# Fused cosformer attention and low-rank mixer: half-head opening, full-array tails, and DMA transposes from batch 2 on

## The chip, the cores and the metric

The kernel runs on one core of one Trainium2 chip. The core has TensorE (PE: matmuls and, on a line of its own, weight loads), VectorE (DVE), ScalarE (ACT), GpSimd (POOL) and SyncE (SP), which here issues the DMAs. The metric is the device time of one execution in microseconds; the time before is the median of three runs.

## The reference

Per batch (8) and head (8), with S = 576 positions and D = 64:

```
r   = max(q or k, 0);  phi = [r * cos(pi/2 * s/S), r * sin(pi/2 * s/S)]      # 128 features
kv  = phi(k)^T v  (128 x 64);   z = sum over s of phi(k)
x   = phi(q) kv / (phi(q) z + 1e-6)                                         # heads side by side: S x 512
A   = U^T x   (32 x 512);   u = x + V^T A
out = u + max(u w1, 0) w2                                                   # w1 512 x 2048, w2 2048 x 512
```

Inputs and output are float32, matmul operands bf16.

## The kernel before

**Tiling.** The 576 positions of a batch are four chunks of 128 (position 4p + c lies on partition p of chunk c) and a tail of 64. Tails of an even batch lie on partitions 0 to 63, of an odd one on 64 to 127, so that two batches, a pair, share one 128-row tail in the MLP. Each batch goes through these units, each a function:

- `load` (L398): six DMAs on SP, a tail and a main part each for k, v and q. k has two buffers, v and q one.
- `k_prep` (L188, on VectorE), `q_prep` (L199, on ScalarE): a cosine and a sine pass per chunk, max(x, 0) times a weight per position. `v_prep` (L173, on GpSimd) casts v and leaves a column of ones, so that kv carries z in column 65.
- `kv_unit` (L210): for four heads, five matmuls each (four chunks and the 64-row tail) into one PSUM tile, cast on VectorE.
- `qtr_unit` (L231): eight TensorE transposes of a chunk of q's features into the PSUM tile T, copied on VectorE to q_pT.
- `x_unit` (L243): eight matmuls of a transposed chunk with kv, then add, reciprocal and multiply on VectorE.
- `A_unit` (L276), `u_unit` (L290): U^T x (a 128 x 32 shape, 64 x 32 for the tail), then V^T A (32 rows) and the add of x on VectorE.
- `utr_unit` (L308): four transposes of u per chunk into T, copied to uT.
- `g1_main` (L327): one of 16 column blocks of the first MLP layer, four matmuls of 512 columns, evicted by ScalarE with a relu into hid (three PSUM buffers g). `g1_tail` (L343): the same for the pair's tail, four blocks at a time. `g2_part` (L364): a quarter of an output chunk's 16 matmuls into o (two PSUM buffers); after the fourth, VectorE adds u (L386) into one of three o_sb buffers, and SP stores it.

PSUM has eight banks: g three, T one, X two (one buffer of two banks), o two.

**Order.** The schedule is manual: each engine and each DMA queue runs its instructions in program order. The opening (L444 to L489) does batch 0 in two halves of four heads, then A, u and transposes, then all 16 `g1_main` of batch 0, and then batch 1's prep, attention and mixer. After that a loop over four pairs (L491) runs 72 MLP slots per pair (`mlp_slots`, L433: 16 and 16 `g1_main`, 4 `g1_tail`, 36 `g2_part`; pair 0 starts at slot 16). Behind a slot it runs the units that `put` has hung there for the next pair's batches: `pe_plan` (L409) gives each unit of a batch an offset, `prep_plan` (L424) those of the prep passes, and `starts` the slot at which a batch begins and the number of slots over which its 36 offsets are spread: (22, 47, 24) in pair 0, (0, 37, 35) later. The next `load` is hung 8 slots behind a batch's start, or at slot 71.

Of the kernel before, what the change touches and what calls it, by code (L numbers as in the profile page):

```python
# [17 lines left out]
def kernel(  # L18
# [14 lines left out]
    H = 8  # L33
# [136 lines left out]
    k_p, q_p, q_pT, kv_sb, x_bf, x_tl, A_sb = {}, {}, {}, {}, {}, {}, {}  # L170
    u_bf, u_tl, uT, uT_tl = {}, {}, {}, {}

    def v_prep(b, h0=0, h1=H):  # L173
        vx = v_ext[b % 2]
        for c in range(4):
            nc.gpsimd.tensor_copy(out=vx[:, c, h0:h1, 0:D], in_=vst[b][:, h0:h1, c, :])  # L176
        if h0 == 0:
            nc.gpsimd.tensor_copy(out=vx[tail(b), 4, :, 0:D], in_=vt[b][tail(b)])
# [9 lines left out]
    def k_prep(b, c, eng, h0=0, h1=H, half=None):  # L188
        if b not in k_p:
            k_p[b] = pool.tile([P, 5, H, 2 * D], BF16, tag="k_p", bufs=1, name="k_p")  # L190
        rows = slice(0, P) if c < 4 else tail(b)
        src = kst[b][:, h0:h1, c, :] if c < 4 else kt[b][rows, h0:h1, :]
        for i, w in enumerate((cosw, sinw)):
            if half in (None, i):
                scaled_relu(
                    eng, k_p[b][rows, c, h0:h1, i * D : i * D + D], src, w[rows, c : c + 1]
                )

    def q_prep(b, c, eng, h0=0, h1=H, half=None):  # L199
        if (b, c) not in q_p:  # L200
            q_p[b, c] = pool.tile([P, H, 2 * D], BF16, tag="q_p", bufs=5, name="q_p")
        rows = slice(0, P) if c < 4 else tail(b)
        src = qst[b][:, h0:h1, c, :] if c < 4 else qt[b][rows, h0:h1, :]
        for i, w in enumerate((cosw, sinw)):
            if half in (None, i):
                scaled_relu(
                    eng, q_p[b, c][rows, h0:h1, i * D : i * D + D], src, w[rows, c : c + 1]
                )

    def kv_unit(b, hg, tag, bufs):  # L210
# [4 lines left out]
        for i in range(4):  # L215
            h = hg * 4 + i
            for c in range(5):
                rows = slice(0, P) if c < 4 else tail(b)
                nc.tensor.matmul(  # L219
                    out=acc[:, i, :],  # L220
                    lhsT=k_p[b][rows, c, h, :],
                    rhs=vx[rows, c, h, :],
                    start=(c == 0),
                    stop=(c == 4),
                )
        nc.vector.tensor_copy(out=kv_sb[b][:, hg * 4 : hg * 4 + 4, :], in_=acc)  # L226

    def cols(c):
        return slice(c * P, c * P + P) if c < 4 else slice(512, S)

    def qtr_unit(b, c, h0=0, h1=H, eng=None):  # L231
        if b not in q_pT:
            q_pT[b] = pool.tile([P, H, S], BF16, tag="q_pT", bufs=1, name="q_pT")
        n = P if c < 4 else TS
        rows = slice(0, P) if c < 4 else tail(b)
        t_ps = ps.tile([P, H, P], BF16, tag="T", bufs=1, name="t_ps")
        for h in range(h0, h1):
            nc.tensor.transpose(  # L238
                out=t_ps[:, h, 0:n], in_=q_p[b, c][rows, h, :], identity=ident[rows, rows]
            )  # L240
        cast(eng or nc.vector, q_pT[b][:, h0:h1, cols(c)], t_ps[:, h0:h1, 0:n])

    def x_unit(b, c, hgs, tag, bufs):  # L243
        if b not in x_bf:
            x_bf[b] = pool.tile([P, 4, DM], BF16, tag="x_bf", bufs=1, name="x_bf")
            x_tl[b] = pool.tile([P, DM], BF16, tag="x_tl", bufs=1, name="x_tl")
        n = P if c < 4 else TS
        rows = slice(0, P) if c < 4 else tail(b)
        ng = len(hgs)
        acc = ps.tile([P, ng, 512], FP32, tag=tag, bufs=bufs, name="x_ps")  # L250
        for g, hg in enumerate(hgs):
            for i in range(4):
                h = hg * 4 + i
                nc.tensor.matmul(  # L254
                    out=acc[rows, g, i * E : i * E + E],
                    lhsT=q_pT[b][:, h, cols(c)],
                    rhs=kv_sb[b][:, h, :],
# [3 lines left out]
        view = acc[rows, :, 0 : 4 * E].rearrange("p g (i e) -> p g i e", e=E)  # L261
        rec = pool.tile([P, ng, 4], FP32, tag="rec", bufs=2, name="rec")
        nc.vector.tensor_scalar(
            out=rec[rows], in0=view[:, :, :, D], scalar1=1e-6, scalar2=None, op0=ALU.add
        )
        nc.vector.reciprocal(out=rec[rows], in_=rec[rows])
        dst = x_bf[b][:, c, :] if c < 4 else x_tl[b][rows, :]
        dst = dst[:, hgs[0] * 256 : hgs[0] * 256 + ng * 256]
        nc.vector.tensor_tensor(  # L269
            out=dst.rearrange("p (g i d) -> p g i d", g=ng, d=D),  # L270
            in0=view[:, :, :, 0:D],
            in1=rec[rows].unsqueeze(3).to_broadcast([n, ng, 4, D]),
# [3 lines left out]
    def A_unit(b, tag, bufs):  # L276
        A_sb[b] = pool.tile([R, DM], BF16, tag="A_sb", bufs=2, name="A_sb")
        a_ps = ps.tile([R, DM], FP32, tag=tag, bufs=bufs, name="a_ps")
        for c in range(5):
            rows = slice(0, P) if c < 4 else tail(b)  # L280
            nc.tensor.matmul(  # L281
                out=a_ps,
                lhsT=U_bf[rows, c, :],
                rhs=x_bf[b][:, c, :] if c < 4 else x_tl[b][rows, :],
# [3 lines left out]
        nc.vector.tensor_copy(out=A_sb[b], in_=a_ps)  # L288

    def u_unit(b, c, tag, bufs):  # L290
        if b not in u_bf:
# [4 lines left out]
        n = P if c < 4 else TS  # L296
        va = ps.tile([P, DM], FP32, tag=tag, bufs=bufs, name="va_ps")
        nc.tensor.matmul(  # L298
            out=va[rows, :], lhsT=V_bf[:, c, 0:n], rhs=A_sb[b], start=True, stop=True
        )  # L300
        nc.vector.tensor_tensor(  # L301
            out=u_bf[b][:, c, :] if c < 4 else u_tl[b // 2][rows, :],
            in0=x_bf[b][:, c, :] if c < 4 else x_tl[b][rows, :],
# [3 lines left out]

    def utr_unit(b, c, eng=None):  # L308
        if b not in uT:
            uT[b] = pool.tile([P, 4, 512], BF16, tag="uT", bufs=2, name="uT")  # L310
            if b % 2 == 0:
                uT_tl[b // 2] = pool.tile([P, 4, P], BF16, tag="uT_tl", bufs=2, name="uT_tl")
        rows = slice(0, P) if c < 4 else tail(b)
        n = P if c < 4 else TS
        t_ps = ps.tile([P, H, P], BF16, tag="T", bufs=1, name="t_ps")
        for d in range(4):
            src = u_bf[b][:, c, :] if c < 4 else u_tl[b // 2][rows, :]
            nc.tensor.transpose(  # L318
                out=t_ps[:, d, 0:n], in_=src[:, d * P : d * P + P], identity=ident[rows, rows]
            )  # L320
        dst = uT[b][:, :, cols(c)] if c < 4 else uT_tl[b // 2][:, :, rows]
        cast(eng or nc.vector, dst, t_ps[:, 0:4, 0:n])
# [4 lines left out]
    def g1_main(b, j):  # L327
# [3 lines left out]
        for d in range(4):  # L331
            nc.tensor.matmul(  # L332
                out=g_ps,
                lhsT=w1_bf[:, d, j * P : j * P + P],
                rhs=uT[b][:, d, :],
# [62 lines left out]
    def load(b):  # L398
        load_alloc(b)
        load_tail(kt[b], k, b)  # L400
        load_main(kst[b], k, b)
        load_tail(vt[b], v, b)
        load_main(vst[b], v, b)
        load_tail(qt[b], q, b)
        load_main(qst[b], q, b)

    V_, A_, G_ = nc.vector, nc.scalar, nc.gpsimd

    def pe_plan(b):  # L409

        plan = []
        for c in range(5):
# [140 lines left out]
```

## Time and profile before

| | |
|---|---|
| median of 3 runs | 414.84 us (414.80 to 415.09) |
| the profiled execution | 414.22 us, of which the span is 412.4 |
| TensorE matmuls busy | 362.8 us, 88% of the span, granted clock 0.961 in the mean |
| weight loads | 183.9 us, 45% |
| VectorE, ScalarE, GpSimd busy | 183.8 us (45%), 141.4 us (34%), 45.7 us (11%) |
| DMA | 46.69 MB, 113 GB/s in the mean |

The profile is of one execution. Its page gives busy times, the chain of waits that ended last, and groups of instructions by line, and the trace behind it answers for any stretch or tile. A matmul's length overlaps its neighbours', so the time that a group of matmuls holds TensorE is read from where the next group starts. A line such as "L219 kv_ps<-v_ext,k_p 128*128 128x65" names the source line, the output, the operands, the array shape (rows * columns of the weights) and the moving operand. In the tables of stretches, the column behind the engines is the granted share of TensorE's clock, then the share of DMA time and GB/s.

### The profile page before, as it was taken

To read this page: it belongs to the slowest core of one execution; us is meant where nothing else is said; L and a number is where in the kernel's file an instruction comes from. 1 tells how busy PE (TensorE), PEld (TensorE's weight loads), DVE (VectorE), ACT (ScalarE), POOL (GpSimd) and SP (SyncE) were. 2 spreads that over 40 slices of the span, in tenths; PEclk is the share of its full clock that TensorE was granted. 3 is DMA by queue.
4 is the path that set the end of the run, shared out by engine and by line. 5 is a ranking of instruction groups with operands and counts; after the bars stand their busy time and mean duration, and the time that the engine had idled before them with its cause. 6 is when DMAs were issued, how large, how long until landed. Compare 5 with 4: busy or idle time off the path is not lost.

```text
span 412.4 us, 6084 instructions
## 1 busy us (share of the span) xinstructions
PE 362.8 (88%) x2544; PEld 183.9 (45%) x2544; DVE 183.8 (45%) x408; ACT 141.4 (34%) x242; POOL 45.7 (11%) x64
## 2 busy tenths in 40 slices
PE   0546797669999994999999999999999999999996
PEld 0322245325564531465356534554475434446442
DVE  2464633564637555534355648352456552000111
ACT  1700268009462000635457005245580002664000
POOL 2453642020000001202000030020000000000000
PEclk9999998559999996999999999999999999999999
DMA  7989783920301139266000491580001121000121
GB/s 198 349 275 326 266 242 93 267 78 1 116 2 51 38 72 292 98 190 183 0 2 25 143 296 61 163 233 2 0 2 52 60 69 51 2 0 2 76 78 77
DMA packets 47533, 46.69 MB, mean 113 GB/s; under 512 B 14065, under 2 KB 38769, under 8 KB 47505
## 3 DMA queue, kind: packets, MB, share of 16 engines
q1 hardware_dynamic: 47504, 46.30, 37.5%
q8 instruction: 20, 0.33, 0.4%
q14 instruction: 9, 0.07, 0.1%
HBM read 36.86 MB, written 9.44 MB: 112 GB/s over the span
## 4 chain that ended last, share of the span: by engine, by line
PE 77%; DVE 14%; DMA 5%; issue 1%; SPq 1%; POOL 1%; DVEq 0%
PE g_ps L332 28%; PE o_ps L375 25%; PE kv_ps L219 5%; PE x_ps L254 4%; PE gt_ps L350 4%; PE va_ps L298 3%; PE t_ps L238 3%; PE t_ps L318 3%; DVE k_p L184 3%; PE a_ps L281 2%; DMA out_dram<-o_sb 2%; DVE q_pT L111 2%; DVE x_bf L269 2%; DVE u_bf L301 2%; DMA kst<-in_k_dram 2%; DMA vst<-in_v_dram 1%
## 5 line engine op out<-in xcount | busy, mean ns | idle before, releaser
L375 PE MATMUL o_ps<-w_bf,hid 128*128 128x512 bf16 x512 | 124.1, 383 | 0.0
L332 PE MATMUL g_ps<-uT,w_bf 128*128 128x512 bf16 x512 | 123.8, 388 | 0.0
L339 ACT ACTIVATE hid<-g_ps 128x512 bf16<-128x512 f32 x128 | 76.5, 597 | 130.5 <-PE g_ps L332 130.5
L332 PEld LDWEIGHTS <-w_bf 128*128 128x128 bf16 x512 | 47.5, 100 | 53.8 <-issue 7.8
L375 PEld LDWEIGHTS <-hid 128*128 128x128 bf16 x512 | 45.7, 98 | 57.5 <-issue 13.4
L386 DVE TENSOR_TENSOR o_sb<-u_bf,o_ps 128x512 f32<-128x512 bf16 x32 | 21.9, 685 | 70.0 <-PE o_ps L375 69.2
L182 ACT ACTIVATE q_p<-qst,cosw 128x512 bf16<-128x512 f32 (+1 forms) x36 | 24.0, 665 | 64.5 <-DMA qst<-in_q_dram 41.7
L176 POOL CAST v_ext<-vst 128x512 bf16<-128x512 f32 (+1 forms) x36 | 20.3, 606 | 213.3 <-DMA vst<-in_v_dram 213.3
L219 PE MATMUL kv_ps<-v_ext,k_p 128*128 128x65 bf16 (+1 forms) x320 | 26.1, 201 | 14.9 <-POOL v_ext L176 9.6
L111 DVE COPY q_pT<-t_ps 128x1024 bf16<-128x1024 bf16 (+2 forms) x45 | 26.1, 579 | 18.8 <-PE t_ps L238 18.4
L254 PE MATMUL x_ps<-kv,q_pT 128*128 128x65 bf16 (+1 forms) x320 | 19.8, 206 | 13.9 <-DVE q_pT L111 12.5
L301 DVE TENSOR_TENSOR u_bf<-x_bf,va_ps 128x512 bf16<-128x512 bf16 x32 | 21.9, 683 | 20.7 <-PE va_ps L298 20.3
L219 PEld LDWEIGHTS <-k_p 128*128 128x128 bf16 (+1 forms) x320 | 19.1, 99 | 24.1 <-DVE k_p L184 14.6
L238 PE MATMUL t_ps<-ident,q_p 128*128 128x128 bf16 (+1 forms) x320 | 26.6, 229 | 0.6 <-DVE q_pT L111 0.6
L254 PEld LDWEIGHTS <-q_pT 128*128 128x128 bf16 (+1 forms) x320 | 15.5, 107 | 25.4 <-DVE q_pT L111 15.9
L238 PEld LDWEIGHTS <-q_p 128*128 128x128 bf16 (+1 forms) x320 | 21.2, 105 | 9.4 <-issue 3.7
L298 PE MATMUL va_ps<-A_sb,V_bf 32*128 32x512 bf16 (+1 forms) x40 | 18.0, 451 | 8.1 <-DVE A_sb L288 7.0
L182 ACT ACTIVATE q_p<-qst,sinw 128x512 bf16<-128x512 f32 (+1 forms) x36 | 23.9, 664 | 0.0
L269 DVE TENSOR_TENSOR x_bf<-x_ps,rec 128x512 bf16<-128x512 f32 (+1 forms) x36 | 22.7, 632 | 1.2
L226 DVE CAST kv<-kv_ps 128x260 bf16<-128x260 f32 x16 | 6.9, 428 | 34.4 <-PE kv_ps L219 34.4
L184 DVE TENSOR_SCALAR k_p<-kst,cosw 128x512 bf16<-128x512 f32 (+1 forms) x36 | 16.1, 447 | 9.8 <-DMA kst<-in_k_dram 9.7
L184 DVE TENSOR_SCALAR k_p<-kst,sinw 128x512 bf16<-128x512 f32 (+1 forms) x36 | 20.1, 559 | 0.0
(45 smaller groups left out, 211.3 us busy)
## 6 DMA issues: line engine op xcount, KB each, us to landing
wst<-in_moe_w_ch_dram SPq DMA_DIRECT2D x8, 1024.0 KB, 6.7
out_dram<-o_sb SPq DMA_DIRECT2D x32, 256.0 KB, 2.3
kst<-in_k_dram SPq DMA_DIRECT2D x7, 1024.0 KB, 7.8
vst<-in_v_dram SPq DMA_DIRECT2D x7, 1024.0 KB, 10.6
qst<-in_q_dram SPq DMA_DIRECT2D x7, 1024.0 KB, 10.2
kt<-in_k_dram SPq DMA_DIRECT2D x8, 128.0 KB, 5.1
vt<-in_v_dram SPq DMA_DIRECT2D x8, 128.0 KB, 8.3
kst<-in_k_dram SPq DMA_DIRECT2D x2, 512.0 KB, 6.5
```

The costliest lines, as they stand in the source:

```text
L111: eng.tensor_copy(out=o, in_=i)
L182: nc.scalar.activation(out=o, in_=i, func=AF.Relu, bias=0.0, scale=w)
L184: eng.tensor_scalar(out=o, in0=i, scalar1=0.0, scalar2=w, op0=ALU.max, op1=ALU.mult)
L219: nc.tensor.matmul(out=acc[:, i, :], lhsT=k_p[b][rows, c, h, :], rhs=vx[rows, c, h, :], start=(c == 0), stop=(c == 4),)
L238: nc.tensor.transpose(out=t_ps[:, h, 0:n], in_=q_p[b, c][rows, h, :], identity=ident[rows, rows])
L254: nc.tensor.matmul(out=acc[rows, g, i * E : i * E + E], lhsT=q_pT[b][:, h, cols(c)], rhs=kv_sb[b][:, h, :], start=True, stop=True,)
L269: nc.vector.tensor_tensor(out=dst.rearrange("p (g i d) -> p g i d", g=ng, d=D), in0=view[:, :, :, 0:D], in1=rec[rows].unsqueeze(3).to_broa ...
L298: nc.tensor.matmul(out=va[rows, :], lhsT=V_bf[:, c, 0:n], rhs=A_sb[b], start=True, stop=True)
L301: nc.vector.tensor_tensor(out=u_bf[b][:, c, :] if c < 4 else u_tl[b // 2][rows, :], in0=x_bf[b][:, c, :] if c < 4 else x_tl[b][rows, :], i ...
L332: nc.tensor.matmul(out=g_ps, lhsT=w1_bf[:, d, j * P : j * P + P], rhs=uT[b][:, d, :], start=(d == 0), stop=(d == 3),)
L339: nc.scalar.activation(out=hid[b][:, j, :], in_=g_ps, func=AF.Relu, bias=0.0, scale=1.0)
L375: nc.tensor.matmul(out=o, lhsT=lhs[:, j, c * P : c * P + P], rhs=w2_bf[:, j, :], start=(j == 0), stop=(j == NJ - 1),)
```

## The change

1. **Full-array tails.** k's, q's and x's tails and their transposes get tiles of their own with 128 partitions (`k_tl`, `q_tl`, `q_tlT`, `x_tl`), zeroed once; U and V are padded with zeros to 128 x 128 blocks, U with one tail block per parity. All matmuls of kv, x, A and u then use 128 x 128 weights.
2. **Opening.** Loads of batch 0 go k, q, v for each half of the heads, tails and U, V on ScalarE's queue; prep is split with cosine on VectorE and sine on ScalarE; denominators have a unit of their own (`den_unit`); uT comes straight from x and A by matmuls that accumulate (`uTd_open`, `uTd_close`), and batch 0's u units move behind the first MLP slots. Batch 1's units are hung on the 16 `g1_main` of batch 0 (`at`), its u units on slots 17 to 21 of pair 0.
3. **DMA transposes.** From batch 2 on, SP issues DMA transposes of q's features (the tail, chunks 0 and 1, chunks 2 and 3) and of u (the same three), in place of `qtr_unit` and `utr_unit`.
4. **Order.** Loads split into k, v and q, hung 1, 3 and 12 slots behind the start of the previous batch's prep; q's passes are closer together; `starts` of pair 0 is (28, 51, 24); A and u units use PSUM tile T.

Core of the diff:

```diff
+    load_tail(kt[0], k, 0, A_)
+    load_tail(qt[0], q, 0, A_)
+    load_tail(vt[0], v, 0, A_)
     for h0 in (0, 4):
         load_main(kst[0], k, 0, h0, h0 + 4)
+        load_main(qst[0], q, 0, h0, h0 + 4)
         load_main(vst[0], v, 0, h0, h0 + 4)
...
+    k_tl = const.tile([P, H, 2 * D], BF16)
+    q_tl = const.tile([P, H, 2 * D], BF16)
+    q_tlT = const.tile([P, H, P], BF16)
+    x_tl = const.tile([P, DM], BF16)
+    U_bf = const.tile([P, 6, P], BF16)
+    V_bf = const.tile([P, 5, P], BF16)
...
                 nc.tensor.matmul(
                     out=acc[:, i, :],
-                    lhsT=k_p[b][rows, c, h, :],
-                    rhs=vx[rows, c, h, :],
+                    lhsT=k_p[b][:, c, h, :] if c < 4 else k_tl[:, h, :],
+                    rhs=vx[:, c, h, :],
...
+    def qtr_dma(b, c0, c1):
+        qT_alloc(b)
+        if c0 < 4:
+            nc.sync.dma_start_transpose(
+                out=q_pT[b][:, c0:c1, :, :].rearrange("f c h t -> f (c h) t"),
+                in_=q_p[b][:, c0:c1, :, :].rearrange("p c h f -> p (c h f)"),
+            )
+        else:
+            nc.sync.dma_start_transpose(
+                out=q_tlT[:, :, tail(b)],
+                in_=q_tl[tail(b), :, :].rearrange("p h f -> p (h f)"),
+            )
...
+    def den_unit(b, hg, tag, bufs):
+        d_ps = ps.tile([P, 5, 4], FP32, tag=tag, bufs=bufs, name="d_ps")
...
+                    rhs=kv_sb[b][:, h, D:E],
...
+    def utr_dma(b, c0, c1):
+        if c0 < 4:
+            uT_alloc(b)
+            nc.sync.dma_start_transpose(
+                out=uT[b][:, c0:c1, :, :].rearrange("m c d t -> m (c d) t"),
+                in_=u_bf[b][:, c0:c1, :].rearrange("p c n -> p (c n)"),
+            )
+        else:
+            uTt_alloc(b // 2)
+            nc.sync.dma_start_transpose(out=uT_tl[b // 2], in_=u_tl[b // 2])
...
+    def uTd_open(b, d, tag, bufs):
...
+        for c in range(4):
+            nc.tensor.matmul(
+                out=t[:, c, :], lhsT=x_bf[b][:, c, d * P : d * P + P], rhs=ident,
+                start=(c == 0), stop=False,
+            )
+    def uTd_close(b, d, eng):
+        t = uT_ps[b, d]
+        nc.tensor.matmul(
+            out=t.rearrange("m c t -> m (c t)"), lhsT=A_sb[b][:, d * P : d * P + P],
+            rhs=V_bf[:, 0:4, :].rearrange("r c t -> r (c t)"), start=False, stop=True,
+        )
+        cast(eng, uT[b][:, :, d, :], t)
...
-                rhs=uT[b][:, d, :],
+                rhs=uT[b][:, :, d, :],
...
+            plan.append((-4, lambda: qtr_dma(b, 4, 5)))
+            plan.append((-2, lambda: qtr_dma(b, 0, 2)))
+            plan.append((0, lambda: qtr_dma(b, 2, 4)))
...
+            plan.append((27, lambda: utr_dma(b, 0, 2)))
+            plan.append((31, lambda: utr_dma(b, 2, 4)))
...
+    for c in ORD:
+        k_prep(0, c, (V_, A_), 0, 4)
+    for c in ORD:
+        q_prep(0, c, (V_, A_), 0, 4)
+    cast_uv()
+    v_prep(0, 0, 4, ORD)
+    for c in ORD:
+        qtr_unit(0, c, 0, 4, A_, "g", 3)
+    kv_unit(0, 0, "T", 1)
+    for c in ORD:
+        k_prep(0, c, (V_, A_), 4, 8)
+    rec0 = den_unit(0, 0, "X", 1)
+    for c in ORD:
+        q_prep(0, c, (V_, A_), 4, 8)
+    v_prep(0, 4, 8, ORD)
+    l1[2]()
+    l1[1]()
+    for c in ORD:
+        qtr_unit(0, c, 4, 8, A_, "g", 3)
+    for c in ORD:
+        xh_unit(0, c, 0, rec0, "o", 2)
+    kv_unit(0, 1, "T", 1)
+    rec1 = den_unit(0, 1, "X", 1)
+    a0 = A_unit(0, "X", 1, A_, 0, 256)
+    for c in ORD:
+        xh_unit(0, c, 1, rec1, "o", 2)
+    for d in range(2):
+        uTd_open(0, d, "g", 3)
+        uTd_close(0, d, A_)
+    uTd_open(0, 2, "g", 3)
+    A_unit(0, "X", 1, V_, 256, 512, a0)
+    uTd_open(0, 3, "o", 2)
+    uTd_close(0, 2, V_)
+    uTd_close(0, 3, A_)
...
+    for n, c in enumerate(ORD):
+        at(n // 2, lambda c=c: k_prep(1, c, (V_, A_)))
+        at(4 + n // 2, lambda c=c: q_prep(1, c, (V_, A_)))
+    for n, c in enumerate(ORD):
+        at(1 + n // 2, lambda c=c: u_unit(0, c, "o", 2))
...
+    at(7, lambda: kv_unit(1, 0, "o", 2), lambda: kv_unit(1, 1, "o", 2))
+    for n, c in enumerate(ORD):
+        at((7, 7, 8, 9, 10)[n], lambda c=c: x_unit(1, c, "X", 1))
+    at(11, lambda: A_unit(1, "o", 2))
...
+        def put_loads(at, b):
+            for n, t in zip((1, 3, 12), loads(b)):
+                put(at + n, t)
...
-                starts = (22, 47, 24)
+                starts = (28, 51, 24)
...
-                        put(w + 8, lambda b=b: load(b + 1))
+                        put_loads(w - (9 if pr == 0 else 6), b + 1)
```

More of the change, by code (lines that the diff above doesn't have):

```diff
@@ L244, in x_unit, with x_alloc, x_of @@
+    def x_alloc(b):
         if b not in x_bf:
             x_bf[b] = pool.tile([P, 4, DM], BF16, tag="x_bf", bufs=1, name="x_bf")
[L246 to L251, printed above, removed]
+    def x_of(b, c, rows=slice(0, P)):
+        return x_bf[b][:, c, :] if c < 4 else x_tl[rows, :]
@@ L260, in x_unit @@
                 )
[L261 to L272, printed above, removed]
+        rec = pool.tile([P, 5, 4], FP32, tag="rec5", bufs=2, name="rec5")
@@ new lines, in uTt_direct @@
+    def uTt_direct(pr, tag, bufs, eng):
+        uTt_alloc(pr)
+        t = ps.tile([P, 4, P], FP32, tag=tag, bufs=bufs, name="uTt_ps")
+        for d in range(4):
+            dd = slice(d * P, d * P + P)
+            nc.tensor.matmul(
+                out=t[:, d, :], lhsT=x_tl[:, dd], rhs=ident, start=(d == 0), stop=False
+            )
+            for i in range(2):
+                nc.tensor.matmul(
+                    out=t[:, d, tail(i)], lhsT=A_sb[2 * pr + i][:, dd],
+                    rhs=V_bf[:, 4, tail(i)], start=False, stop=(d == 3 and i == 1),
+                )
+        cast(eng, uT_tl[pr], t)
```

359 lines of the change are left out of this document (215 added, 144 removed).

## Prediction

> **What bounds the kernel now.** I read the table of stretches first, cut where the kernel's own stages begin: batch 0's attention and mixer, then batch 0's first MLP layer and batch 1's attention, then the second half of pair 0, then pairs 1, 2 and 3.
>
> ```profile
> 0.00:48.09 48.09, 21.18 (x151) 11.29 (x151) 23.29 (x73) 12.37 (x27) 18.82 (x32) 1.00 0.91 282
> 48.09:91.06 42.97, 33.18 (x216) 16.68 (x215) 21.61 (x42) 16.15 (x27) 13.77 (x13) 0.76 0.65 187
> 91.06:175.41 84.35, 75.93 (x574) 38.51 (x573) 47.06 (x105) 29.93 (x50) 4.16 (x5) 0.94 0.28 82
> 175.41:261.02 85.61, 85.06 (x637) 43.65 (x636) 44.43 (x95) 33.83 (x56) 6.01 (x10) 1.00 0.39 112
> 261.02:346.19 85.17, 85.17 (x638) 43.77 (x637) 40.58 (x85) 27.60 (x46) 2.90 (x5) 1.00 0.24 70
> 346.19:412.40 66.21, 62.28 (x337) 30.02 (x334) 6.87 (x10) 21.49 (x36) 0.00 (x0) 0.99 0.11 40
> ```
>
> The columns are length, busy time of TensorE, weight loads, VectorE, ScalarE and GpSimd, granted clock, DMA share, GB/s. TensorE is busy all through pairs 1 and 2 at full clock: there only TensorE work counts. It is 44% busy in the first 48 us, where DMA is 91% busy, and the clock falls to 0.76 in the second stretch: there latency counts.
>
> Pair 3 has no attention beside it. Its last output is evicted here (the chain of waits):
>
> ```profile
> 346.19 27.63 PE g_ps L332 x128
> 408.51 0.69 DVE o_sb L386
> ```
>
> So 72 MLP slots alone take 408.51 - 346.19 = 62.3 us, 0.865 us each. Pairs 1 and 2 take 85.6 and 85.2 for the same slots plus two batches of attention and mixer: (85.6 - 62.3) / 2 = 11.65 us of TensorE a batch.
>
> What that batch is made of, in the TensorE timeline of pair 2 (start, length, line, tile, shape, count):
>
> ```profile
> 263.19 1.50 PE L219 MATMUL kv_ps<-v_ext,k_p 128*128 128x65 bf16 x20
> 264.63 1.04 PE L332 MATMUL g_ps<-uT,w_bf 128*128 128x512 bf16 x4
> 265.50 0.61 PE L238 MATMUL t_ps<-ident,q_p 128*128 128x128 bf16 x8
> 265.95 1.03 PE L332 MATMUL g_ps<-uT,w_bf 128*128 128x512 bf16 x4
> 270.43 0.42 PE L254 MATMUL x_ps<-kv,q_pT 128*128 128x65 bf16 x8
> 270.69 1.02 PE L332 MATMUL g_ps<-uT,w_bf 128*128 128x512 bf16 x4
> 284.15 1.04 PE L281 MATMUL a_ps<-x_bf,U_bf 128*32 128x512 bf16 x4
> 285.12 0.39 PE L281 MATMUL a_ps<-x_tl,U_bf 64*32 64x512 bf16 x1
> 285.44 1.90 PE L332 MATMUL g_ps<-uT,w_bf 128*128 128x512 bf16 x8
> 287.27 0.39 PE L298 MATMUL va_ps<-A_sb,V_bf 32*128 32x512 bf16 x1
> 287.59 1.90 PE L332 MATMUL g_ps<-uT,w_bf 128*128 128x512 bf16 x8
> 290.61 0.39 PE L318 MATMUL t_ps<-ident,u_bf 128*128 128x128 bf16 x4
> 290.83 1.03 PE L332 MATMUL g_ps<-uT,w_bf 128*128 128x512 bf16 x4
> ```
>
> Starts are to be subtracted, since lengths overlap. Eight x matmuls of 65 columns take 270.69 - 270.43 = 0.26 us, 33 ns each. Twenty kv matmuls of the same width should take 0.65 and take 264.63 - 263.19 = 1.44. A kv unit goes to the 64-row tail and back four times: 0.79 / 8 = 0.1 us per change of array shape. The mixer shows the same: a va matmul is 0.216 of streaming (0.865 / 4; eight g_ps from 285.44 end at 287.17), then 0.1 before and 0.1 behind it.
>
> **The change, part by part.** *Full-array tails*, batches 2 to 7. A batch loses 2 x 0.79 (kv), about 0.2 (x tail, two changes), 0.2 (A: 285.44 - 284.15 = 1.29 for five matmuls of 0.216) and 5 x 0.2 (va): 3.0 us.
>
> *Transposes off TensorE*, batches 2 to 7. A q transpose unit takes 265.95 - 265.50 = 0.45, five of them 2.25; a u unit 290.83 - 290.61 = 0.22, five about 1.15. Together 3.4 us a batch, and VectorE loses ten evictions, which costs or gives nothing as VectorE is half idle.
>
> A batch then costs 11.65 - 6.4 = 5.25 us, a pair 62.3 + 10.5 = 72.8: **-12.8** in pair 1, **-12.4** in pair 2, 0 in pair 3. The first MLP layer now reads uT in runs of 128 columns; the trace has no such matmul. Its ends are nothing, and what 128-column matmuls cost: 3.57 us for 64 gt_ps is 56 ns, four are 7 ns over 0.216, times 512 is 3.6 us.
>
> ```profile
> 373.82 3.57 PE gt_ps L350 x64
> ```
>
> I take nothing.
>
> *Second half of pair 0* now lasts 84.35. Pure, it is 56 slots x 0.865 = 48.4, two batches at 5.25, and batch 1's five u units that move here (1.1): 60.0, **-24.4**. That also removes this wait:
>
> ```profile
> 159.10 0.48 DVE L184 TENSOR_SCALAR k_p<-kst,cosw 128x512 bf16<-128x512 f32 x1 [7.02 <-DMA kst<-in_k_dram]
> 161.35 0.58 PE L298 MATMUL va_ps<-A_sb,V_bf 32*128 32x512 bf16 x1 [5.48 <-DVE A_sb L288]
> ```
>
> Batch 4's k load came late, VectorE stood on it with A_sb queued behind, TensorE waited 5.48 us. In the new order the k load is issued one slot after the previous batch's prep begins, 15 slots ahead of its use.
>
> *Opening.* Batch 0 needs 3.54 MB, and U and V 0.15.
>
> ```profile
> 0.00:10.00 10.00, 0.23 (x2) 0.23 (x3) 3.04 (x13) 1.68 (x3) 1.93 (x12) 1.00 0.74 193
> 10.00:20.00 10.00, 6.00 (x55) 3.83 (x54) 4.75 (x18) 8.30 (x20) 4.25 (x11) 1.00 1.08 349
> ```
>
> ```profile
> 14.53 0.49 ACT L182 ACTIVATE q_p<-qt,cosw 64x256 bf16<-64x256 f32 x1
> 14.93 0.49 ACT L182 ACTIVATE q_p<-qt,sinw 64x256 bf16<-64x256 f32 x1
> ```
>
> At 193, then 349 GB/s all of it has landed at 15.0 us. The prep of each half is split, cosine on VectorE and sine on ScalarE; ScalarE, which also evicts the q transposes, is the longer: from about 7.0 (first k half landed, tables ready behind seven DMA issues on ScalarE's own queue) ten sine halves at the 0.40 cadence of the rows above, five evictions, ten more halves and five more evictions at 0.5 (the evictions of uT last 0.598): 7 + 4 + 2.5 + 4 + 2.5 = 20.0.
>
> ```profile
> L109 ACT ACTIVATE uT<-t_ps 128x512 bf16<-128x512 bf16 x4 | 2.4, 598 | 25.3 <-PE t_ps L318 25.3
> L226 DVE CAST kv<-kv_ps 128x260 bf16<-128x260 f32 x16 | 6.9, 428 | 34.4 <-PE kv_ps L219 34.4
> L269 DVE TENSOR_TENSOR x_bf<-x_ps,rec 128x256 bf16<-128x256 f32 x8 | 3.4, 424 | 0.3
> ```
>
> Behind it: kv of the second half 1.4 and its eviction 0.43, denominators with their four small VectorE operations 1.8, five multiplies of 0.424, A and its eviction 1.0, the direct uT and its eviction 1.0: 20.0 + 7.7, say 28. The ten u and transpose steps that before stood between A and the first MLP matmul are behind it now.
>
> Then 16 MLP slots with batch 1 in their gaps. In the first eight ScalarE is longest: 8 evictions of hid at 0.5, 10 sine passes at 0.61 (713 ns less the 0.1 by which such passes overlap), 3 wide transpose evictions at 1.0 (twice the 0.5), 13 us. Behind: kv 1.5, five x units one after the other through the one X buffer at 1.65 (x_ps at 109.96 and 111.61), A and its eviction 2, direct uT and the last slots 4: 16. The second half of pair 0 starts at 28 + 29 = 57 instead of 91.06: **-34**.
>
> ```profile
> L182 ACT ACTIVATE q_p<-qst,sinw 128x512 bf16<-128x512 f32 x28 | 20.0, 713 | 0.0
> ```
>
> ```profile
> 109.96 0.43 PE L254 MATMUL x_ps<-kv,q_pT 128*128 128x65 bf16 x8 [0.36 <-DVE x_bf L269]
> 111.61 0.43 PE L254 MATMUL x_ps<-kv,q_pT 128*128 128x65 bf16 x8 [0.36 <-DVE x_bf L269]
> ```
>
> *What the DMA transposes add.* The trace has none. Two chunks of q are 512 KB, read in runs of 256 bytes as the q, k and v tails are. DMA in 255 to 300 us, slices of 1.1 us:
>
> ```profile
> GB/s 233 0 0 184 49 0 35 207 173 277 340 342 237 341 347 201 301 339 217 30 8 0 15 0 0 0 0 0 0 0 0 0 0 0 0 0 0 0 0 0
> kst<-in_k_dram SPq DMA_DIRECT2D x1, 1024.0 KB, 6.7
> vst<-in_v_dram SPq DMA_DIRECT2D x1, 1024.0 KB, 10.6
> kt<-in_k_dram SPq DMA_DIRECT2D x1, 128.0 KB, 3.2
> ```
>
> ```profile
> 263.03 0.62 SPq L71 DMA_DIRECT2D kst<-in_k_dram  x1
> ```
>
> The dips to about 200 GB/s are the tails passing among 340 GB/s of main loads. At 200, 512 KB take T = 2.6 us; at 340, 1.5, the lower end; if nothing overlaps, four times the tail's 3.2 us, 12.8, the upper end. I take 2.6, the row of the same run length. [...]
>
> These transposes stand on SP's queue behind the next batch's k and v loads, and behind them on SP stand output stores. SP waits there for ScalarE's q passes, later for VectorE's u adds; three o_sb buffers, 3.46 us apart, cover about 10 us of it. The u transposes have 20 slots or more before their reader. The q ones don't: in an odd batch the k load goes out about slot 30, v lands 12.4 us later (three issues of 0.6 ahead of it, as in the SP row above, then 10.6), the first pair of chunks T later, 15.0; its x unit stands 12 slots on, 0.865 each plus kv, 11.3: 3.7 us of wait. Chunks 2 and 3 land T later, their x units 4.0 later: no more. For even batches of pairs 1 and 2 only the q load is ahead: 1 us each. For batch 2 spacing is tighter and w1, w2 and three batches' loads, over 20 MB, press: 8. For batch 3, 3. Batch 7 has no loads ahead: 0. Sum 8 + 3 + 1 + 3.7 + 1 = **+17**.
>
> Against the profiled execution: 412.4 - 34 - 24.4 - 12.8 - 12.4 + 17 = 345.8 of span. It took 414.22, 1.8 over its span; the median of the runs, 414.84, is 0.6 more. Forecast 347.6, say 348.
>
> **The rivals.**
> - *The transposes find idle DMA.* SP runs ahead of TensorE, so loads go out earlier than I count. DMA share of 0.24 to 0.39 in pairs 1 and 2 speaks for it. Most of the 17 goes: 331.
> - *The opening is held by DMA.* 11.4 MB (batches 0 and 1, U, V, w1) must land before the last quarter of w1 is used; at the first stretch's 282 GB/s that is 40 us, but buffers make loads wait for casts. Second half of pair 0 at 70: 361.
> - *Transposes at T = 6.* First x unit of six batches 3.4 later, third 2.0 later: 6 x 5.4 = 32, so 380.
> - *Slower than before.* The transposes are so slow that each q transpose holds TensorE. Extra time is 6 x ((T - 2.6) + (T - 4.0)); it eats all 67 us gained from T = 8.9. At the upper end of 12.8 it is 114, so 462, beyond the time before. For it: one tail alone takes 3.2 us to land; against it: in the dips tails overlap. [...]
>
> **How the numbers follow.** Forecast 0.55, no collision 0.14, held opening 0.10, T near 6 0.13, slower 0.08. The range 328 to 385 takes in the first four with the bounds on run length and opening. The ends of T beyond 6 are left out, with the 0.08. About 0.2%, or 0.8 us, is what a measurement can tell from no change. Faster 0.91, same 0.01 (T just at break-even), slower 0.08.
>
> **What would show it.** Right: the first g_ps at about 28 us, slot 16 at about 57, kv units of 20 matmuls in 0.65 us, pairs 1 and 2 near 73 us plus waits of x_ps on DMA q_pT totalling about 17, and transposes of q landing 3 to 15 us after issue. Wrong: x_ps waits above 60 us in total, SP held for longer than 9 us a transpose, kv units still above 1 us, or the first g_ps after 35.

## The result, and the profile after

The changed kernel takes 383.6 us, the median of 4 runs (382.93 to 385.05), beside 414.86 for the kernel before (4 runs, 414.8 to 415.09): a ratio of 0.925, 95% interval 0.922 to 0.9281. The forecast was 348, so of a gain of 67 us 31 came. The profiled run took 382.93, its span is 381.1.

The stretches of the changed kernel, cut at the first g_ps of each stage, with the columns of the table in the prediction (length, TensorE, weight loads, VectorE, ScalarE, GpSimd, granted clock, DMA share, GB/s):

```profile
0.00:39.30 39.30, 17.53 (x191) 13.95 (x192) 16.45 (x53) 15.86 (x36) 15.08 (x35) 1.00 1.00 288
39.30:71.73 32.43, 25.34 (x228) 13.77 (x227) 23.81 (x41) 17.84 (x29) 14.18 (x11) 1.00 0.92 278
71.73:147.35 75.62, 63.32 (x459) 31.58 (x457) 42.23 (x89) 30.46 (x51) 6.39 (x10) 0.95 0.72 173
147.35:230.87 83.52, 75.15 (x518) 37.81 (x516) 34.48 (x76) 33.92 (x56) 5.74 (x10) 0.96 0.62 153
230.87:314.76 83.89, 74.30 (x518) 37.74 (x516) 30.50 (x65) 27.58 (x46) 2.90 (x5) 0.94 0.49 99
314.76:381.00 66.24, 62.44 (x337) 30.06 (x335) 6.87 (x10) 21.49 (x36) 0.00 (x0) 1.00 0.12 41
```

Set against the terms of the sum:

| stretch | predicted, us | measured | difference |
|---|---|---|---|
| opening | 28 | 39.3 | +11.3 |
| first 16 slots, batch 1's attention | 29 | 32.4 | +3.4 |
| pair 0's rest, with waits of 8 + 3 | 71.0 | 75.6 | +4.6 |
| pair 1, with waits of 1 + 3.7 | 77.5 | 83.5 | +6.0 |
| pair 2, with a wait of 1 | 73.8 | 83.9 | +10.1 |
| pair 3 and end | 66.2 | 66.3 | +0.1 |

Before, TensorE was busy 85.06 of the 85.61 us of pair 1; now 75.15 of 83.52. The work has left TensorE and the time has not followed: TensorE now waits. The idle time of TensorE by its releaser (total, times, longest) has one large new row, and the timeline has its places. In brackets stands the wait ahead of the instruction:

```profile
PE x_ps L340 <- DMA q_pT<-q_p: 24.5, 5, 9.1
```

```profile
124.94 0.62 PE L340 MATMUL x_ps<-kv,q_pT 128*128 128x65 bf16 x8 [7.04 <-DMA q_pT<-q_p]
...
159.83 0.62 PE L340 MATMUL x_ps<-kv,q_pT 128*128 128x65 bf16 x8 [5.93 <-DMA q_pT<-q_p]
...
200.03 0.48 PE L340 MATMUL x_ps<-kv,q_pT 128*128 128x65 bf16 x8 [1.93 <-DMA q_pT<-q_p]
...
246.51 0.62 PE L340 MATMUL x_ps<-kv,q_pT 128*128 128x65 bf16 x8 [9.09 <-DMA q_pT<-q_p]
246.95 3.60 PE L468 MATMUL g_ps<-uT,w_bf 128*128 128x512 bf16 x8
250.34 0.65 PE L340 MATMUL x_ps<-kv,q_pT 128*128 128x65 bf16 x8
```

These are batches 3, 4, 5 and 6; batch 2 waits nothing, batch 7 0.50. Behind these waits TensorE is also slow for a while: from 246.95 to 250.34 eight g_ps take 3.39 us instead of 8 x 0.216 = 1.73. The granted clock is 0.50 there, from 246.5 to 251.4. Counted in this way, behind each of the four waits 1.4 to 2.4 us are lost, some 7 in all, so the DMA transposes cost about 32 us where 17 were forecast.

The queue of SyncE ahead of the longest wait (start, time of the issue):

```profile
221.59 0.67 SPq L81 DMA_DIRECT2D kt<-in_k_dram  x1
222.31 0.62 SPq L75 DMA_DIRECT2D kst<-in_k_dram  x1
223.03 0.66 SPq L81 DMA_DIRECT2D vt<-in_v_dram  x1
223.73 0.62 SPq L75 DMA_DIRECT2D vst<-in_v_dram  x1
224.85 3.51 SPq L529 DMA_DIRECT2D out_dram<-o_sb  x1
228.46 3.00 SPq L417 DMA_TRANSPOSE uT<-u_bf  x1
231.56 0.53 SPq L529 DMA_DIRECT2D out_dram<-o_sb  x1
232.14 2.60 SPq L417 DMA_TRANSPOSE uT<-u_bf  x1
234.84 0.63 SPq L81 DMA_DIRECT2D qt<-in_q_dram  x1
235.56 0.58 SPq L75 DMA_DIRECT2D qst<-in_q_dram  x1
236.23 0.53 SPq L529 DMA_DIRECT2D out_dram<-o_sb  x1
236.85 1.79 SPq L276 DMA_TRANSPOSE q_tlT<-q_tl  x1
238.69 7.84 SPq L271 DMA_TRANSPOSE q_pT<-q_p  x2
```

TensorE stood at batch 6's first x unit from 237.4 on (246.51 - 9.09). Its q transposes were issued at 238.69, behind batch 7's k, v and q loads, three output stores and batch 5's mixer transposes; the prediction had only the q load ahead of an even batch. The first q transposes of batches 3, 4 and 6 were issued 2.5, 1.3 and 1.3 us after TensorE had come to a stand for them, and then took another 4.5, 4.6 and 7.8 us to land; the shortest of the twelve took 4.3. An issue is not free either: an ordinary load holds SyncE for 0.6 us, a transpose here for 1.8 and more.

### The profile page after: what moved, and what is told of

Its sections match the earlier page's. It is cut to its first block, busy times and chain, and to the rows that moved or that the text cites. A ratio compares the mean times of both kernels' runs of the same rounds, so it can differ in the third digit from the quotient of the medians.

```text
span 381.1 us, 5516 instructions
## 1 busy us (share of the span) xinstructions
PE 318.1 (83%) x2241; PEld 164.9 (43%) x2241; DVE 154.3 (40%) x332; ACT 147.2 (39%) x254; POOL 44.3 (12%) x70
## 4 chain that ended last, share of the span: by engine, by line
PE 59%; DMA 14%; DVE 12%; ACT 6%; SPq 5%; issue 2%; POOL 1%; ACTq 1%; POOLq 0%
PE g_ps L468 26%; PE o_ps L511 24%; DMA q_pT<-q_p 7%; DVE k_p L209 4%; ACT q_p L207 3%; DMA st_uv<-in_moe_U_dram 3%; DMA wst<-in_moe_w_ch_dram 3%; PE x_ps L340 3%; PE kv_ps L241 2%; PE a_ps L366 2%; PE va_ps L383 2%; DVE u_bf L384 2%; PE gt_ps L486 1%; DMA out_dram<-o_sb 1%; SPq L271 1%
## 5 line engine op out<-in xcount | busy, mean ns | idle before, releaser
L475 ACT ACTIVATE hid<-g_ps 128x512 bf16<-128x512 f32 x128 | 76.1, 596 | 128.4 <-PE g_ps L468 128.4
L340 PE MATMUL x_ps<-kv,q_pT 128*128 128x65 bf16 x224 | 12.7, 202 | 28.4 <-DMA q_pT<-q_p 24.5
L292 DVE TENSOR_SCALAR rec<-x_ps 128x8 f32<-128x8 f32 (+1 forms) x35 | 5.8, 166 | 60.4 <-PE x_ps L340 60.4
L340 PEld LDWEIGHTS <-q_pT 128*128 128x128 bf16 x224 | 10.6, 103 | 37.9 <-DMA q_pT<-q_p 27.2
L115 DVE CAST kv<-kv_ps 128x260 bf16<-128x260 f32 x16 | 6.8, 428 | 32.4 <-PE kv_ps L241 32.4
L350 DVE TENSOR_TENSOR x_bf<-x_ps,rec 128x512 bf16<-128x512 f32 x28 | 19.4, 691 | 1.0
L207 ACT ACTIVATE q_tl<-qt,cosw 64x512 bf16<-64x512 f32 x6 | 4.3, 717 | 39.2 <-DMA qt<-in_q_dram 39.1
L383 PE MATMUL va_ps<-A_sb,V_bf 128*128 128x512 bf16 x40 | 15.0, 378 | 4.9 <-DVE u_tl L384 1.9
L207 ACT ACTIVATE q_p<-qst,cosw 128x512 bf16<-128x512 f32 x24 | 17.1, 713 | 4.4 <-issue 2.6
L115 POOL CAST w_bf<-wst 128x2048 bf16<-128x2048 f32 x8 | 15.6, 1950 | 14.2 <-DMA wst<-in_moe_w_ch_dram 14.2
L511 PE MATMUL o_ps<-w_bf,hid_tl 128*128 128x512 bf16 x64 | 16.1, 395 | 0.0
L486 PE MATMUL gt_ps<-uT_tl,w_bf 128*128 128x128 bf16 x256 | 15.3, 219 | 0.0
## 6 DMA issues: line engine op xcount, KB each, us to landing
vst<-in_v_dram SPq DMA_DIRECT2D x7, 1024.0 KB, 10.1
```

The costliest lines, as they stand in the source:

```text
L115: eng.tensor_copy(out=o, in_=i)
L207: nc.scalar.activation(out=o, in_=i, func=AF.Relu, bias=0.0, scale=w)
L340: nc.tensor.matmul(out=acc[:, g, i * E : i * E + E], lhsT=qT_of(b, c, h), rhs=kv_sb[b][:, h, :], start=True, stop=True,)
L350: nc.vector.tensor_tensor(out=x_of(b, c, rows).rearrange("p (g i d) -> p g i d", g=2, d=D), in0=view[:, :, :, 0:D], in1=rec[rows].unsqueez ...
L383: nc.tensor.matmul(out=va, lhsT=V_bf[:, c, :], rhs=A_sb[b], start=True, stop=True)
L475: nc.scalar.activation(out=hid[b][:, j, :], in_=g_ps, func=AF.Relu, bias=0.0, scale=1.0)
```

## The experiments

The times of e1 to e4 stand beside a kernel before of 414.81 us, those of e5 to e8 beside 414.55, e9 to e11 beside 415.36; stages are counted from the first eviction of hid in each.

**e1: both transposes back on TensorE.**

```diff
-    BY_DMA = True
+    BY_DMA = False
```

> All transposes of batches 2 to 7 back on TensorE (q and mixer output), tails and opening as in the changed kernel. Theory (queue): the DMA transposes cost 24.5 us of waits of x_ps and about 6.5 us of half clock behind the long ones, and save 3.4 us of TensorE in each of six batches, 20 us; without them the kernel takes about 371 us, with pairs 1 and 2 near 79.6 us each and no wait of x_ps above 1 us. Rival (the waits come from late loads and preps, not from the transposes): the waits stay under other names and the 20 us come on top, 390 to 403 us.

The flag also puts the A and u units back into PSUM tile X and spaces q's passes as before, so e1 differs in a little more than the transposes.

Measured: 375.38 us, ratio 0.9039 (0.9008 to 0.907), where 371 was expected. The DMA transposes lose against TensorE in this order of the queue. Pairs 1 and 2:

```profile
148.11:228.51 80.40, 78.04 (x629) 43.53 (x634) 44.14 (x94) 34.28 (x57) 5.12 (x9) 1.00 0.38 112
228.51:308.33 79.82, 77.93 (x627) 43.46 (x632) 40.47 (x84) 27.93 (x46) 0.61 (x1) 1.00 0.12 42
```

About 80.1 us against 85.4 before is what is left of the gain without the DMA transposes, in the main the full-array tails: 2.65 us a batch, beside 3.0 forecast. The pairs are within 0.8 us of the 79.6 expected. Most of what is missing to 371 lies ahead of them: the first 16 slots took 34.4 us instead of 32.2 in the changed kernel by the same cut, and pair 0's rest 74.4 instead of 75.6, though its wait of 7.04 is gone.

**e2: the next batch's loads behind the q transposes, from pair 1 on.**

```diff
                     for o, t in prep_plan(b):
...
-                        put_loads(w - (9 if pr == 0 else 6), b + 1)
+                        put_loads(w - 9 if pr == 0 else w, b + 1)
                 for o, t in pe_plan(b):
                     put(w + round(o * starts[2] / 36), t)
+                if pr > 0 and b == nb:
+                    put_loads(w, b + 1)
...
-                put_loads(58, nb + 3)
```

> Transposes stay on the DMA queue; only the loads of the next batch that stood ahead of the q transposes of batches 4, 5 and 6 on SyncE's queue are issued behind them. Theory (queue order): the waits of batches 4, 5 and 6 (5.93, 1.93 and 9.09 us) and the half clock behind them go, pairs 1 and 2 near 73 to 75 us, 362 us in all; the wait of batch 3 (7.04) stays. Rival (a transpose is slow by itself, or the outputs and the mixer's transposes hold it): each wait stays within 2 us of what it was, 381 to 384 us.

Measured: 366.57 us, ratio 0.8839 (0.8808 to 0.887): 17 us less than the changed kernel, and not one transfer fewer. The waits of batches 4, 5 and 6 are now 1.95, 0.72 and 0.68, batch 3's is 6.86. All waits on q transposes, then pairs 1 and 2:

```profile
PE x_ps L340 <- DMA q_pT<-q_p: 10.7, 5, 6.9
148.80:227.07 78.27, 73.59 (x511) 37.45 (x516) 34.29 (x75) 33.93 (x56) 5.74 (x10) 0.98 0.69 170
227.07:300.24 73.17, 71.69 (x512) 36.93 (x517) 30.52 (x65) 27.59 (x46) 2.90 (x5) 1.00 0.56 130
```

Pair 2 comes near the 72.8 that was forecast for it without waits, and DMA has the same bytes to move. The rival falls: the twelve q transposes take as long as before, 4.7 us from issue to landing in the median and 4.6 in the changed kernel; they are issued earlier. The 362 us expected were not reached, since pair 1 stays above the 73 to 75 expected: 4.4 us of waits are left in it, 1.7 of them on VectorE.

**e4: q on TensorE, the mixer output by DMA.**

```diff
-        if BY_DMA:
-            plan.append((-4, lambda: qtr_dma(b, 4, 5)))
-            plan.append((-2, lambda: qtr_dma(b, 0, 2)))
-            plan.append((0, lambda: qtr_dma(b, 2, 4)))
-        else:
+        if True:
             for c in range(5):
```

> Only the q transposes of batches 2 to 7 go back to TensorE (five units of 0.45 us a batch); the mixer's stay on the DMA queue. Theory (it is the q transposes, read 12 slots behind their issue, that cost; the mixer's have 20 slots and more): all 31 us of waits and half clock go and 13.5 us of TensorE come back, 365 us, faster than with all transposes on TensorE. Rival (any transposes on the queue delay the loads and outputs): preps wait for loads in their place, 375 us or more.

Measured: 366.0 us, ratio 0.882 (0.8789 to 0.8851), as expected. No x_ps waits on a DMA. Pair 2 takes 76.1: set against e1, with the differences named there, the mixer's transposes by DMA are worth (79.8 - 76.1) / 2 = 1.85 us a batch, q's (76.1 - 73.2) / 2 = 1.45 in e2 or, without its remaining 1.17 us of waits, 2.0.

**e7: the q transposes on ScalarE's queue.**

```diff
-            nc.sync.dma_start_transpose(
+            nc.scalar.dma_start_transpose(
```

(twice, in `qtr_dma`.)

> The changed kernel with the q transposes issued on ScalarE's queue, behind ScalarE's own sine and cosine passes, instead of on SyncE's behind loads, stores and the mixer's transposes. Theory (place in SyncE's queue): the waits of x_ps on q_pT fall from 24.5 to 8 us or less, while ScalarE is held 1.2 to 5 us an issue, which stalls evictions of hid in even batches: 366 to 376. Rival (the DMA engines, or the wait of every issue for the landing of the eighth before it, set the time of a transpose wherever it is issued): waits of 18 us and more, and ScalarE's stalls on top, 384 to 395.

Measured: 389.59 us, ratio 0.9389 (0.9358 to 0.942), outside what the theory expected. The waits of x_ps fell to 5.7 us in all, but that alone doesn't show that place in SyncE's queue made them, since TensorE now waits 25.3 us for hid, in part ahead of the same x units. ScalarE's evictions of hid stand behind its issues (pair 1; ACTq is ScalarE's queue):

```profile
146.84 1.28 ACTq L276 DMA_TRANSPOSE q_tlT<-q_tl  x1
148.22 6.14 ACTq L271 DMA_TRANSPOSE q_pT<-q_p  x2
154.41 1.57 ACT L475 ACTIVATE hid<-g_ps 128x512 bf16<-128x512 f32 x3 [10.58 <-DMA q_pT<-q_p]
```

TensorE then waits for hid, 8.06 us at 155.05 and 13.75 at 249.72. I had priced ScalarE's hold by the issues, 1.2 to 5 us; what counts is that the first of them is issued only at 146.84, when the mixer's transpose on SyncE's queue, issued at 140.44, has landed 6.3 later. The program makes a transpose on one queue wait for those on the other, and SyncE's next one, in turn, goes out at 156.60, when the last q transpose has landed, 4.3 us after its issue at 152.3. So e7 does not separate the DMA engines from this ordering; e2 does.

**e3: the opening's order.** The angle tables ahead of all but two of ScalarE's DMA issues, U and V behind batch 0's loads on SyncE, their casts behind batch 0's v casts. The three moves are made at once, and no run separates them.

```diff
     load_tail(kt[0], k, 0, A_)
     load_tail(qt[0], q, 0, A_)
+    nc.scalar.activation(out=sinw, in_=iota, func=AF.Sin, bias=0.0, scale=scale_ang)
+    nc.scalar.activation(out=cosw, in_=iota, func=AF.Sin, bias=halfpi, scale=-scale_ang)
...
+        if h0 == 0:
+            load_tail(vt[0], v, 0)
...
-    A_.dma_start(out=stV, in_=moe_V)
+    nc.sync.dma_start(out=stV, in_=moe_V)
...
-    cast_uv()
     v_prep(0, 0, 4, ORD)
...
     v_prep(0, 4, 8, ORD)
+    cast_uv()
```

> Only the opening is changed: the angle tables are made on ScalarE behind two DMA issues instead of seven, U and V are loaded behind batch 0 on SyncE's queue, and their casts stand behind batch 0's v casts on GpSimd. Theory (a DMA issue waits for the landing of the eighth one before it, and the tables wait behind such issues): the first pass on k at about 8.5 instead of 12.6 us, the first g_ps at 34 to 36 instead of 39.3, 378 us. Rival (the 3.7 MB of batch 0, U and V set the opening): first g_ps at 38 to 40, 382 to 384 us.

Measured: 377.78 us, ratio 0.9107 (0.907 to 0.9145). ScalarE in the changed kernel:

```profile
2.88 0.95 ACTq L133 DMA_DIRECT2D st_uv<-in_moe_U_dram  x1
7.09 1.15 ACTq L137 DMA_DIRECT2D st_uv<-in_moe_U_dram  x2
10.63 0.34 ACTq L138 DMA_DIRECT2D st_uv<-in_moe_V_dram  x1
11.00 1.28 ACT L155 ACT_TABLE_LOAD   x1 [11.00 <-DMA qt<-in_q_dram]
...
12.60 0.49 ACT L207 ACTIVATE k_tl<-kt,sinw 64x256 bf16<-64x256 f32 x1
```

and in e3:

```profile
2.16 1.28 ACT L143 ACT_TABLE_LOAD   x1 [2.16 <-issue]
...
6.62 0.51 ACT L208 ACTIVATE k_tl<-kt,sinw 64x256 bf16<-64x256 f32 x1 [2.76 <-DMA kt<-in_k_dram]
```

The first four issues went out back to back; the last three wait, the first two of them until 7.09 and V until 10.63, and the tables behind them. In the trace each DMA carries the number of the semaphore that it raises on landing. Eight numbers (100, 102 to 108) go round over both queues, and a DMA that gets a number again waits until the one that had it has landed: the first U tail for the k tail (issued at 0.73, landed 6.3 later), V for the q tail (issued at 1.49, landed 9.1 later). In e3 the first pass comes 6.0 earlier and the first g_ps at 31.7 instead of 39.3, both earlier than the 8.5 and 34 to 36 expected. Of the 7.6 us 5.8 reach the end; batch 5 now waits 4.21 instead of 1.93 for its q transposes.

**e11: without the first cast of w1** (its quarter of the weights set to zero, 512 hidden columns left out).

```diff
-    w1_cast(0, wst[0], G_)
...
+    G_.memset(w1_bf[:, :, 0:512], 0.0)
```

> The changed kernel without GpSimd's cast of the first quarter of w1; that part of the weights is zero instead, so 512 of the 2048 hidden columns are left out of the result. Theory (GpSimd's cast slows the passes of VectorE that run beside it): four k cosine passes of the second half of batch 0 take 1.13 us instead of 2.76, and the first g_ps comes 1.3 to 1.7 earlier, at about 37.8. Rival (the passes wait for their k data): they stay above 2.3 us, first g_ps at 39.0 to 39.6.

Measured, in one run: 376.16 us, first g_ps at 33.3. VectorE's k passes beside GpSimd's cast in the changed kernel, which runs from 20.71 to 22.71, and without it in e11:

```profile
20.60 2.76 DVE L209 TENSOR_SCALAR k_p<-kst,cosw 128x256 bf16<-128x256 f32 x4
```

```profile
19.58 1.12 DVE L210 TENSOR_SCALAR k_p<-kst,cosw 128x256 bf16<-128x256 f32 x4
```

For the passes the theory holds: 2.76 against 1.12. The first g_ps came 4.5 us earlier than the 37.8 expected. Matmuls behind the passes ran at full pace here (four a_ps in 0.61 us, 1.06 in the changed kernel); why they did in this run is not shown, so its whole gain is not the cast's. The next experiment is on the pace.

**e6 and e8: q on TensorE with the opening of e3, and the same with TensorE kept busy.** e6 is e3 and e4 together; e8 adds 109 matmuls without a reader:

```diff
+    def warm(n):
+        for _ in range(n):
+            nc.tensor.matmul(
+                out=spare["t"][:, 1, 0:P], lhsT=ident, rhs=ident, start=True, stop=True
+            )
...
     v_prep(0, 0, 4, ORD)
+    warm(64)
...
         xh_unit(0, c, 0, rec0, "o", 2)
+        warm(3)
```

> q transposes on TensorE, the mixer's on the DMA queue (e4), with the opening of e3. Theory (the two effects have different places and add): 366.0 less 6 to 8.6 is 357.4 to 360, with slot 16 of pair 0 near 64 and no wait of x_ps on a DMA. Rival (the earlier start only reaches batch 2's loads earlier, and VectorE waits for them): the second half of pair 0 grows from 72.3 by over 4 us, 362 to 366.

> e6 with 109 added 128x128 matmuls in the opening, whose results nothing reads: 64 before the first q transposes, the others in gaps where TensorE waits for evictions. Theory (the opening's matmuls run at half pace because TensorE was idle before them, four uT_ps matmuls of 128 columns in 0.63 us): the quartets take 0.39 us or less, and the first g_ps comes 2 to 3 us earlier than in e6, 355 to 357. Rival (the pace isn't set by that, and the chain of evictions sets the opening): quartets still at 0.6, first g_ps within 1 us of e6's, 357 to 361.

Measured: e6 359.25 us, ratio 0.865 (0.8626 to 0.8674), so the opening and the q transposes add up as expected. e8 359.62, ratio 0.8666 (0.8637 to 0.8695): no gain. The opening did get its part, though less than expected. The same matmuls in e6:

```profile
27.81 0.61 PE L433 MATMUL uT_ps<-ident,x_bf 128*128 128x128 bf16 x4
...
31.77 1.54 PE L469 MATMUL g_ps<-uT,w_bf 128*128 128x512 bf16 x5
```

and in e8:

```profile
27.36 0.39 PE L450 MATMUL uT_ps<-ident,x_bf 128*128 128x128 bf16 x4
...
30.20 2.18 PE L486 MATMUL g_ps<-uT,w_bf 128*128 128x512 bf16 x8
```

Four of them take 0.39 us instead of 0.61 where TensorE wasn't idle before, and the first g_ps comes 1.6 earlier. Then ScalarE meets batch 2's q load before it has landed, with evictions of hid queued behind, and pair 0's rest takes 76.7 us instead of 72.9:

```profile
72.35 0.72 ACT L208 ACTIVATE q_p<-qst,cosw 128x512 bf16<-128x512 f32 x1 [2.01 <-DMA qst<-in_q_dram]
```

The pace comes back after some us: behind the wait of 9.09 the granted clock is 0.50 until 251.4, some 5 us, and behind that of 1.93 for 3.4 us. The length of the wait does not decide by itself whether it falls: batch 5's wait of only 1.93 us is followed by eight o_ps in 3.39 (200.32 to 203.71, clock 0.50), and in e5, below, a wait of 2.07 us that ends at 132.49 by four o_ps in 1.71, another of 2.07 that ends at 112.66 by four in 0.87 (granted clock 0.90 in the mean from 120 to 137, 1.00 from 100 to 120). In the opening the column of granted clocks doesn't tell: it reads 1.00 from 20.80 to 31.70 in e6, where most matmuls went at half pace; four uT_ps take 0.61 to 0.64 us up to 29.50 and 0.39 at 30.57.

**e5, e9, e10: all transposes by DMA, in a better order.** e5 is e2 and e3 together, and batch 4's loads also go behind batch 3's q transposes; e9 adds the matmuls of e8; e10 puts batch 4's prep three slots earlier.

```diff
-                        put_loads(w - 9 if pr == 0 else w, b + 1)
+                        put_loads(w - 9 if b == 2 else w, b + 1, 4 if b == 3 else 12)
...
-                    put(58 + o, t)
+                    put((63 if pr == 0 else 58) + o, t)
```

> All transposes of batches 2 to 7 on the DMA queue, with the opening of e3, the loads of e2 behind the q transposes, and also batch 4's k, v and q loads behind batch 3's q transposes (prep of batch 4 five slots later for it). Theory (queue order alone makes the waits): 383.6 less 17 (e2), less 6 to 8 (opening), less 4 to 7 for batch 3's wait and the half clock behind it: 350 to 356. Rival (the time only moves: batch 4's loads come late for its prep, or output stores and the mixer's transposes, which still stand ahead, hold batch 3's q transposes): batch 3's wait stays above 5 us or a wait of VectorE on DMA kst of more than 3 us appears, 358 to 364.

> e5 with the 109 added matmuls of e8 in the opening. In e8 they brought slot 16 of pair 0 forward by 1.8 us, and a wait of ScalarE for batch 2's q load ate it. Theory (the gain of the opening holds where the loads come in time, as in e5): slot 16 near 61.5 and 353.5 to 354.5 us. Rival (the time moves to batch 2's or 4's loads again): 355 to 357.

> e9 with the prep of batch 4 at slots 60 to 65 of pair 0 instead of 63 to 68. Theory (in e5 VectorE's k passes of batch 4 stood between the mixer's adds of batch 3 and cost TensorE a wait of 2.07 us on u_bf and the half pace behind it, about 3.5 us): that wait shrinks below 1 us, 350 to 352. Rival (three slots earlier the k passes wait for the k load instead): a wait of VectorE on DMA kst or kt of over 1.5 us, 354 us or more.

Measured: e5 355.68 us, ratio 0.8578 (0.8549 to 0.8607), within the theory's range. Batch 3's wait falls from 7.04 to 2.07. e9 353.37, ratio 0.8531 (0.8497 to 0.8565): the lowest of all here, 30 us under the changed kernel and 0.1 below what its theory expected, though its interval overlaps e5's, so those two are not told apart.

e10 356.08, ratio 0.8558 (0.8523 to 0.8593): no gain. TensorE's wait for VectorE that it was to remove shrank from 1.72 us (e9) to 1.21, while batch 3's wait grew to 3.02 and ScalarE's waits for batch 2's q load, which the edit doesn't touch, cost TensorE 2.54 and 2.19. Neither theory is borne out: the time lies where the rival put it, but VectorE's wait for a k load, which was to be its cause, is not there. The runs of e10 and e9 spread by 1.3 and 1.7%, wider than the effect sought.

## Why the prediction was right in direction and wrong in size

*Right.* Full-array tails: a kv unit takes 0.61 us (149.68 - 149.07), forecast 0.65, before 1.44.

```profile
149.07 0.29 PE L241 MATMUL kv_ps<-v_ext,k_p 128*128 128x65 bf16 x4
...
149.68 1.89 PE L468 MATMUL g_ps<-uT,w_bf 128*128 128x512 bf16 x8
```

The transposes leave TensorE: e1 against e2 gives (79.8 - 73.2 + 1.2) / 2 = 3.9 us a batch, forecast 3.4. Pair 2 without its waits: 72.0 in e2, forecast 72.8. T: the q transposes of batch 7, behind no load, in slices of 0.4 us from 276 on (178 to 220 in slices 17 to 29 are theirs, with a gap between the two, the 355 behind them are output stores):

```profile
GB/s 0 0 0 0 0 0 0 122 150 56 0 0 0 0 0 0 178 214 209 220 218 201 71 101 217 207 218 216 202 313 355 261 389 118 20 26 20 0 0 0
```

They move at 200 to 220 GB/s, the rate taken from the tails; 512 KB are 2.4 us at 215, forecast 2.6. That is the transfer alone: from issue to landing the twelve took 4.3 to 7.8 us, within the 3 to 15 named beforehand. The slower rival, which needs T above 8.9, falls with that 2.4. The wait on A_sb fell from 5.48 to 0.9, and pair 3 is as it was, 66.24 us beside 66.21. The matmuls on runs of 128 columns cost nothing: pair 3 would show it.

*Wrong: "for even batches of pairs 1 and 2 only the q load is ahead: 1 us each".* They measured 5.93 and 9.09, batch 3 7.04 instead of 3, batch 2 0 instead of 8, batch 5 1.93 instead of 3.7. The sum of 17 for 24.5 looks nearer than its parts were, by luck: the 8 for batch 2 that did not come makes up for about half of what batches 3, 4 and 6 took beyond theirs. I had counted the loads ahead of an odd batch and left out, for the even ones, that at a pair's boundary the other batch's loads, three stores and two mixer transposes come together on one queue, each waiting its own turn. e2 shows it: same transfers, other order, 17 us less. To the waits came the half pace behind them, which had no term in the sum: about 7 us.

*Wrong: "tables ready behind seven DMA issues on ScalarE's own queue", first k pass at 7.0.* I priced seven issues at their own 0.6 us. Three of them wait for landings; the first pass ran at 12.60, 5.6 late, and in e3 at 6.62. Behind that, from 25.6 by the sum's own lengths to 27.4 measured, comes VectorE slowed by GpSimd's cast (2.76 us for four passes, 1.12 in e11). The step "20.0 + 7.7" measured 11.9 instead of 7.7, from 27.4 to 39.3: matmuls at half pace, and evictions that wait for them in turn. In e11, where the pace was full from about 25.6 on, the same step took 8.5, from 24.8 to 33.3, so some 3.3 of the 4.2 us go with the pace; this rests on one run. In e8, with TensorE kept busy, 1.6 came back against e6. The rest was not tried. Of the signs named beforehand, a first g_ps after 35 is the one of being wrong that came.

*Smaller.* The first 16 slots took 32.4 for 29, in part 1.91 us on VectorE's u add, which no experiment isolates. In pair 0 the pure 60 us left out short waits on evictions, 4.7 us together between 82 and 141. The "over 20 MB" behind the 8 us of batch 2 are 19.0 by their shapes (w1 and w2 8.4, three batches 10.6).

Of the rivals none came true as written. "The opening is held by DMA" put pair 0's second half at 70, and it began at 71.7, but for another reason: e3 moves the same bytes and has it 8.6 us earlier. "Transposes at T = 6" put the kernel at 380, near the 383.6 measured, but not by its cause: e2 loses most of the waits with the time from issue to landing unchanged.

## What to carry to other kernels

Work taken off the busiest engine became latency somewhere else here, 24.5 us of waits: before forecasting the gain, write down the queue that carries it in program order, with every load, store and transpose ahead of the one that is waited for, at the worst place (here a pair's boundary), with the 4 to 8 us that a transpose here took from issue to landing, and add what the half pace costs that can follow a wait of TensorE (here 1.4 to 2.4 us behind each of four). A transpose that is read soon belongs ahead of loads that are needed late (17.0 us in e2), and if it can't stand there, on TensorE (17.6 us in e4). DMA issues with compute behind them on the same engine were cheap here, 0.66 to 0.95 us each, only as long as none of them had to wait for a landing; of the three that had to, the last held the tables until 11.00.

## What the runs showed of the hardware beyond that

VectorE passes from SBUF to SBUF took 2.76 us for four beside GpSimd's cast of a quarter of w1 (128x2048) in the changed kernel and 1.12 without it in e11. A DMA transpose of 512 KB held SyncE's queue for 1.3 to 5.8 us, where a plain load mostly held it for 0.6; shortest, median and longest in ns of the twelve of q in the changed kernel:

```profile
L271 SPq DMA_TRANSPOSE q_pT<-q_p x12: 1317/2038/5772, 81.7 to 284.2; - x12
```

Why it varies so much was not settled; the longest is the one at 238.69, issued 3.1 us behind batch 7's q load.
